# First attention: P divided by its sum on GpSimd ahead of the transpose, V as the stationary side of PV, and a new planner table

## The chip, the core and the metric

The kernel runs on one core of a Trainium2 chip. The metric is the time of one execution in device microseconds (us), taken as the median of several runs. The engines are named as in the profile: PE (TensorE: matmuls, transposes; PEld is its weight loads), DVE (VectorE), ACT (ScalarE), POOL (GpSimd) and SP (SyncE, which issues the loads).

## The reference

Two attention blocks share one shape and run over different caches. Their results are joined along the last axis.

```python
# B=16 batches, Sq=32 queries, D=1024, 32 query heads, Sk=1024 cached keys, Dh=128; all bf16
def block(x, k_cache, v_cache, wq, wo):
    q = heads(x @ wq)                                 # (B, 32, Sq, Dh)
    scores = einsum("bhqd,bhkd->bhqk", q, k) * Dh**-0.5
    p = softmax(scores)
    o = einsum("bhqk,bhkd->bhqd", p, v)
    return merge(o) @ wo                              # (B, Sq, D)
# A: 4 KV heads, each used by 8 query heads.   B: 32 KV heads, one for each query head.
return concatenate([A, B], axis=-1)
```

The K and V caches of B are 2 x 134 MB, those of A 2 x 17 MB, and the weights another 34 MB. Nearly all of the traffic is read once.

## The kernel before

**Units of work.** The first attention (A) is cut into 128 quads: one batch, four query heads and their 32 queries make 128 rows, against 1024 keys. `quadA_all` (L1239) lists the steps of one: the K tile is transposed on PE for every second quad (`st_ktrA`, L969), scores go to two PSUM banks (`st_scoresA`, L995), DVE takes the row maximum (`st_max`, L1038), ACT makes the exponential and its row sum (`st_exp`, L1051), PE transposes P in four pieces that each move two bf16 as one f32 (`st_ptr`, L1063), ACT or DVE copies that to SBUF (`st_pev`, `evac` L651), PE multiplies by V (`st_pvA`, L1083), DVE takes the reciprocal of the row sum (`st_recip`, L1165), ACT or DVE scales O by it (`st_norm`, L1174 or L1175), PE transposes O (`st_otr`, L1182), and the result is copied to `OTA_sb` (`evac` L651). In `st_pvA` the transposed P is the stationary side and V the moving one, so that O comes out with queries on the partitions, and `st_otr` has to turn it.

The second attention (B) is cut into 64 pairs of quads (`pairB`). Each takes four K tiles, which DVE transposes in 32x32 blocks (`st_ktrB`, L976), and four V tiles; its steps are `st_scoresB` (L1027), `st_max`, `st_exp`, `st_ptB` (L1097), `st_pvB` (L1116), `st_recip`, `st_norm` and `st_otr` (L1190). The last pair uses `st_last` (L1135, L1157) in place of `st_pvB` and what follows. Around both stand the projections of Q (`qprojA_head` L735, `qprojB` L754), the shuffle of Q for B (`qprepB_tr` L765, `qprepB_sh` L778) and the output projections (`oproj` L823, added up on DVE at L835, L844 and L839).

**The order.** `Prog.add` records every step with the buffers that it reads and writes. `list_schedule` then places all of them once, before the program is built: it keeps a planned time for each engine, takes durations from the table `DUR`, hands out the buffers of `SLOTS` (eight PSUM banks, two buffers of `P` and so on), chooses ACT or DVE for a step marked "any", and ranks what is ready by one of the 16 settings in `RANKS`. Which setting holds for each run of 77 steps is read from the table `TUNE`. What comes out is one fixed sequence for each engine, joined by semaphores. An engine works through its sequence in order, so a step that waits holds up all that stands behind it on that engine.

**The loads.** All loads are issued by SP, also in the planned order: KB (L910), VB (L955), KA (L891), VA (L898), weights (L714, L795, L805). A load waits until the last reader of its buffer is done, and the loads behind it wait with it. The outputs of all but the last group are issued by POOL (L847), the last by SP (L841).

The accumulated row sum and its reciprocal lie in `stat`, a buffer of eight slots with four columns, one slot for each quad:

```python
SLOTS = {"bank": 8, "P": 2, "P2": 1, "PT": 2, "PT2": 2, "stat": 8, "O": 2, "O2": 3}
```

## Time and profile before

| | |
|---|---|
| median of 3 runs | 852.57 us (852.47 to 854.04) |
| profiled execution | 851.34 us, of which the span from first to last instruction is 849.5 us |
| granted TensorE clock, mean | 0.995 |
| busy time | PE 783.0 us, DVE 727.0, ACT 623.6, POOL 6.1 |
| bytes moved | 341.68 MB, mean 402 GB/s |
| maximum, L1038 | 256 x 1210 ns on DVE |
| exponential, L1051 | 256 x some 1120 ns on ACT, and 205 ns each to read out the sum |
| K transposes of B, L976 | 256 x 1222 ns on DVE |
| norm of A, L1174 and L1175 | 123 x 378 ns on ACT, 5 x 327 ns on DVE |
| reciprocal, L1165 | 256 x 145 ns on DVE |
| copy of A's transposed O, L651 | 128x64 f32, 111 x 225 ns on ACT, 17 x 214 ns on DVE |
| transpose of A's O, L1182 | 128 matmuls, 225 ns each from start to end |

How to read it: the profile gives each instruction's duration from start to end. Matmuls overlap, so PE's own pace is read from the chain of waits, where each step is counted until the next. A duration on an engine costs time only where something later waits for it. The windows list, for a stretch of the span, the busy time of PE, PEld, DVE, ACT and POOL, the granted clock of PE, the DMA engines' share and GB/s.

### The profile page before, as it was taken

The numbers are of one execution on the slowest core, as the hardware profiler recorded it, in microseconds if no ns is written. First come the engines' busy times: TensorE is split into PE (matmuls) and PEld (weight loads), VectorE is DVE, ScalarE is ACT, GpSimd is POOL, SyncE is SP. The second block draws the span as 40 slices with busy tenths as digits, with TensorE's granted clock in tenths as the row PEclk, the third lists the DMA queues.
The fourth block names the chain that finished last, engine by engine and source line by source line (L and its number), as shares of the span: only waits on it lengthen the run. The fifth ranks groups of instructions, "written<-read, shape, count | busy, mean of one in ns | idle before, by whom it ended". The sixth has DMA issues, their size and how long they took to land.

```text
span 849.5 us, 29749 instructions
## 1 busy us (share of the span) xinstructions
PE 783.0 (92%) x13056; PEld 522.6 (62%) x13056; DVE 727.0 (86%) x1018; ACT 623.6 (73%) x1363; POOL 6.1 (1%) x20
## 2 busy tenths in 40 slices
PE   7989999999898999998999988999899998899878
PEld 4456665666565566665666665666666666666655
DVE  1499987979799898987999898998999978998995
ACT  3497787778677777786788787677877867686874
POOL 1000000000000000000000000000000000000000
PEclk9999999999999999999999999999999999999999
DMA  9999999999999999999999999999999999999995
GB/s 339 415 412 414 411 411 410 405 393 394 416 384 412 409 395 415 416 398 412 414 392 408 411 392 416 415 416 405 410 402 415 412 414 415 415 400 414 416 418 226
DMA packets 112208, 341.68 MB, mean 402 GB/s; under 512 B 12048, under 2 KB 12304, under 8 KB 112080
## 3 DMA queue, kind: packets, MB, share of 16 engines
q1 hardware_dynamic: 111520, 337.95, 100.0%
q8 instruction: 103, 1.69, 0.7%
q0 software_dynamic: 560, 1.84, 0.5%
q14 instruction: 25, 0.20, 0.1%
HBM read 337.64 MB, written 2.10 MB: 400 GB/s over the span
## 4 chain that ended last, share of the span: by engine, by line
PE 55%; DVE 23%; ACT 14%; DMA 5%; issue 2%; SPq 1%; DVEq 0%; ACTq 0%
DVE stat L1038 10%; PE psum L1116 10%; PE psum L823 10%; DVE KB_sb L976 8%; ACT P_sb L1051 8%; PE psum L1027 6%; PE psum L1063 5%; PE psum L754 5%; PE psum L1097 5%; PE psum L1083 4%; DMA KB_sb<-in_B_k_cache_dram 4%; PE psum L995 4%; PE psum L735 4%; ACT PT_sb L651 2%; ACT O_sb L1174 1%
## 5 line engine op out<-in xcount | busy, mean ns | idle before, releaser
L1038 DVE TENSOR_REDUCE stat<-psum 128x1 f32<-128x1024 f32 x256 | 303.6, 1210 | 50.7 <-PE psum L995 31.5
L1051 ACT ACTIVATE P_sb<-psum,stat 128x1024 bf16<-128x1024 f32 x246 | 275.9, 1122 | 63.2 <-DVE stat L1038 59.7
L976 DVE STREAM_TRANSPOSE KB_sb<-KB_sb 128x1024 f32<-128x1024 f32 x240 | 286.6, 1222 | 6.2 <-DMA KB_sb<-in_B_k_cache_dram 6.0
L651 ACT COPY PT_sb<-psum 128x512 f32<-128x512 f32 x226 | 131.4, 604 | 35.2 <-PE psum L1063 22.0
L1116 PE MATMUL psum<-VB_sb,PT_sb 64*64 64x256 bf16 x3584 | 116.2, 271 | 8.6 <-ACT P_sb L1051 5.2
L1116 PEld LDWEIGHTS psum<-VB_sb,PT_sb 64*64 64x64 bf16 x3584 | 97.0, 107 | 27.7 <-issue 25.5
L1174 ACT ACTIVATE O_sb<-psum,stat 128x128 bf16<-128x128 f32 (+1 forms) x205 | 80.8, 417 | 43.2 <-PE psum L1083 23.1
L1063 PE MATMUL psum<-id,P_sb 128*128 128x128 f32 x512 | 88.7, 297 | 6.9 <-ACT P_sb L1051 4.1
L1063 PEld LDWEIGHTS psum<-id,P_sb 128*128 128x128 f32 x512 | 74.0, 208 | 25.2 <-ACT P_sb L1051 13.8
L995 PE MATMUL psum<-KTA_sb,QT_sb 128*128 128x512 bf16 x256 | 84.4, 384 | 3.1 <-ACT P_sb L1051 1.6
L1083 PE MATMUL psum<-VA_sb,PT_sb 128*128 128x128 bf16 x1024 | 78.8, 221 | 7.5 <-ACT P_sb L1051 2.6
L1083 PEld LDWEIGHTS psum<-VA_sb,PT_sb 128*128 128x128 bf16 x1024 | 63.2, 99 | 31.6 <-issue 12.0
L1027 PE MATMUL psum<-KB_sb,QR 32*32 32x512 bf16 x3840 | 73.3, 394 | 8.1 <-ACT P_sb L1051 4.6
L1097 PE MATMUL psum<-id,P_sb 128*128 128x128 f32 x472 | 76.2, 287 | 4.1 <-ACT P_sb L1051 3.5
L754 PE MATMUL psum<-wq_sb,xT_sb 128*128 128x512 bf16 x256 | 72.4, 394 | 3.3 <-DMA wq_sb<-in_B_wq_dram 1.6
L1097 PEld LDWEIGHTS psum<-id,P_sb 128*128 128x128 f32 x472 | 63.8, 193 | 17.3 <-ACT P_sb L1051 7.5
L823 PE MATMUL psum<-woB_sb,OTB_sb 128*128 128x512 bf16 x256 | 66.9, 380 | 2.4 <-ACT P_sb L1051 1.7
L1027 PEld LDWEIGHTS psum<-KB_sb,QR 32*32 32x32 bf16 x3840 | 43.8, 89 | 35.3 <-ACT P_sb L1051 8.3
L823 PE MATMUL psum<-woA_sb,OTA_sb 128*128 128x512 bf16 x256 | 62.8, 380 | 0.4 <-ACT OTA_sb L651 0.3
L735 PE MATMUL psum<-xT_sb,wq_sb 128*128 128x512 bf16 x192 | 54.2, 380 | 1.7 <-issue 1.2
L1051 ACT ACTIVATION_READ_ACCUMULATOR P_sb<-psum,stat 128x1 f32 x246 | 50.3, 205 | 0.0
L835 DVE TENSOR_TENSOR acc<-acc,psum 128x512 f32<-128x512 f32 x64 | 41.3, 675 | 9.6 <-PE psum L823 9.4
(74 smaller groups left out, 720.2 us busy)
## 6 DMA issues: line engine op xcount, KB each, us to landing
KB_sb<-in_B_k_cache_dram SPq DMA_DIRECT2D x240, 512.0 KB, 8.9
VB_sb<-in_B_v_cache_dram SPq DMA_DIRECT2D x234, 512.0 KB, 7.8
KA_sb<-in_A_k_cache_dram SPq DMA_DIRECT2D x64, 256.0 KB, 7.8
VA_sb<-in_A_v_cache_dram SPq DMA_DIRECT2D x64, 256.0 KB, 8.0
wq_sb<-in_B_wq_dram SPq DMA_DIRECT2D x16, 512.0 KB, 8.3
woB_sb<-in_B_wo_dram SPq DMA_DIRECT2D x32, 256.0 KB, 8.5
woA_sb<-in_A_wo_dram SPq DMA_DIRECT2D x32, 256.0 KB, 7.0
wq_sb<-in_B_k_cache_dram SPq DMA_DIRECT2D x16, 512.0 KB, 11.5
```

The lines of the kernel that those rows point to most:

```text
L651: return e.copy(dst, src) if hasattr(e, "activation") else e.tensor_copy(dst, src)
L754: last = e.matmul(bank(v)[:, 0:CW], xT_sb[:, 1, j, G * P:(G + 1) * P], wq_sb[:, j, mh * CW:(mh + 1) * CW], start=(j == 0), stop=(j == DJ - 1))
L823: last = e.matmul(bank(v)[:, 0:OUTW], OT[:, gp, hh, :], wo_[:, hh, oh * OUTW:(oh + 1) * OUTW], start=(hh == 0), stop=(hh == nh - 1))
L976: pr.add("dve", lambda e: e.transpose(tile_k(x).bitcast(F32), tile_k(x).bitcast(F32)), writes=[home_k(x)], name="KBt_tr", rtag={home_k(x): ...
L995: pr.add("pe", lambda e, u=u: e.matmul(bank(vS[u]), qt[:, q.b, q.hh0:q.hh0 + 4, :].rearrange("p a q -> p (a q)"), KTA_sb[:, sl, u * 512:(u ...
L1027: last = e.matmul(bank(q.vS[g2])[32 * x:32 * x + 32, :].rearrange("p (s j) -> p s j", s=16), lhsT, rhs, start=(fp == 0), stop=(fp == 3), t ...
L1038: pr.add("dve", lambda e: e.tensor_reduce(stat[:, vst.idx, 0:1], both(vS), AXIS.XY, ALU.max, negate=True), writes=vS + [vst], name="max")
L1051: return e.activation(dst, src, ACTF.Exp, bias=stat[:, vst.idx, 0:1], scale=1.0, accum_out=stat[:, vst.idx, 1:2])
L1063: last = e.transpose(bank(vb)[:, m * P:(m + 1) * P], p32[:, m:Sk // 2:NPK], id32[:])
L1083: last = e.matmul(bank(vb)[:, 0:Dh], ptc_of(vPT, c, 0, P), VA_sb[:, kvs, c, :], start=(c == 0), stop=(c == NCH - 1))
L1097: last = e.transpose(bank(vb)[:, m * P:(m + 1) * P], p32[:, 4 * h + m:Sk:8], id32[:])
L1116: last = e.matmul(bank(q.vbo)[n0:n0 + 64, 0:2 * Dh].rearrange("p (i d) -> p i d", i=2), pt2_chunk(vPT, c, e0, n0), v2[e0:e0 + 64, :, c, :] ...
```

## The change

For the first attention, the reciprocal of the row sum is taken straight after the exponential, and POOL multiplies the 128x1024 P by it in place, ahead of the transpose. P gets three buffers. In `st_pvA` V becomes the stationary side and the transposed P the moving one, so that O comes out with the head dimension on the partitions: A's norm and the transpose of O are gone, and one copy of 128x128 takes O to `OTA_sb`.

Along with it: in B the two row sums of a pair share a slot of a new buffer `rs`, and one reciprocal serves both; the transpose of B's O has a moving side of 64 columns in place of 128; the shuffle of Q for B uses a stationary side of 64 columns (`idd`) and half as many matmuls, and the transpose ahead of it is made in place. The planner has other durations for these steps (1.2 us and 0.2 of hand-off for the multiplication), another table `TUNE`, and finer turns behind step 4466. As every step is placed anew, the order on each engine differs nearly throughout.

```diff
-SLOTS = {"bank": 8, "P": 2, "P2": 1, "PT": 2, "PT2": 2, "stat": 8, "O": 2, "O2": 3}
+SLOTS = {"rs": 4, "bank": 8, "P": 3, "P2": 1, "PT": 2, "PT2": 2, "stat": 8, "O2": 3}
...
-TUNE = (6, 7, 1, 5, 6, 8, 8, 8, 8, 8, 8, 11, 5, 15, 1, 9, 0, 1, 5, 1, 7, 14,
...
+TUNE = (12, 6, 6, 13, 3, 12, 12, 14, 4, 15, 6, 2, 15, 11, 15, 5, 15, 7, 14, 2, 0, 5,
...
+FINE = 4466
+FINE_WINDOW = 11
...
-            turn = len(order) // WINDOW
+            turn = len(order) // WINDOW if len(order) < FINE else FINE // WINDOW + (len(order) - FINE) // FINE_WINDOW
...
...
         def qprepB_tr(m_, G):
-            pr.add("dve", lambda e: e.transpose(QBt[:, :].bitcast(F32), Qtok[:, qs, :].bitcast(F32)),
+            pr.add("dve", lambda e: e.transpose(Qtok[:, qs, :].bitcast(F32), Qtok[:, qs, :].bitcast(F32)),
...
         def qprepB_sh(m_, G):
-                    for rg in range(4):
-                        last = e.matmul(out_[32 * rg:32 * rg + 32], ident[32 * a:32 * a + 32, 32 * a:32 * a + 32], src_[:, rg // 2, :, :],
-                                        start=True, stop=True, tile_position=(32 * a, 32 * rg))
+                    for hf in range(2):
+                        last = e.matmul(out_[64 * hf:64 * hf + 64], idd[32 * a:32 * a + 32, :], src_[:, hf, :, :],
+                                        start=True, stop=True, tile_position=(32 * a, 64 * hf))
...
         def st_exp(q):
-                return e.activation(dst, src, ACTF.Exp, bias=stat[:, vst.idx, 0:1], scale=1.0, accum_out=stat[:, vst.idx, 1:2])
+                return e.activation(dst, src, ACTF.Exp, bias=stat[:, vst.idx, 0:1], scale=1.0, accum_out=stat[:, vst.idx, 1:2] if q.pi == 0 else rs[:, q.vrs.idx, q.e:q.e + 1])
...
         def st_pvA(q):
-                    last = e.matmul(bank(vb)[:, 0:Dh], ptc_of(vPT, c, 0, P), VA_sb[:, kvs, c, :], start=(c == 0), stop=(c == NCH - 1))
+                    last = e.matmul(bank(vb)[:, 0:P], VA_sb[:, kvs, c, :], ptc_of(vPT, c, 0, P), start=(c == 0), stop=(c == NCH - 1))
...
         def st_otr(q):
             if q.pi == 0:
-                pr.add("pe", lambda e: e.transpose(bank(vb)[:, 256:320].bitcast(BF), O_sb[:, vO.idx, :], ident[:]), reads=[vO, "ident"], writes=[vb], name="OT_tr")
-                dst = OTA_sb[:, gp, q.hh0:q.hh0 + 4, :].bitcast(F32)[:, :, tb // 2:(tb + Sq) // 2]
-                src = lambda: bank(vb)[:, 256:320].rearrange("p (a q) -> p a q", a=4)
+                dst = OTA_sb[:, gp, q.hh0:q.hh0 + 4, tb:tb + Sq]
+                src = lambda: bank(vb)[:, 0:P].rearrange("p (a q) -> p a q", a=4)
             else:
-                        last = e.matmul(bank(vb)[:, 256:384], O2_sb[:, vO.idx, i, :], rowsel[:, i, :], start=(i == 0), stop=(i == 1))
+                        last = e.matmul(bank(vb)[:, 256 + 64 * i:320 + 64 * i].rearrange("p (t q) -> p t q", t=2), O2_sb[:, vO.idx, i, :], sel(i), start=True, stop=True)
...
         def quadA_all(q):
             st_exp(q)
+            st_recip(q)
+            pr.add("pool", lambda g: g.tensor_scalar(P_sb[:, vP.idx, :], P_sb[:, vP.idx, :], stat[:, vst.idx, 2:3], 1.0, ALU.mult, ALU.mult),
+                   reads=[vst, "idd"], writes=[vP], name="pnorm")
             st_ptr(q)
             st_pev(q)
             st_pvA(q)
-            st_recip(q)
-            st_norm(q)
             st_otr(q)
```

In the changed kernel's own numbering, the multiplication is L1270, the transposes of A's P are L1072, A's PV is L1092, B's PV is L1125, the K transposes of A are L977 and those of B L984, the reciprocals L1174 (A) and L1176 (B), the additions L843, L852 and L847.

## The prediction

> **What bounds the kernel now.** I read the page first: the shares, the slices and the chain.

> ```profile
> PE 783.0 (92%) x13056; PEld 522.6 (62%) x13056; DVE 727.0 (86%) x1018; ACT 623.6 (73%) x1363; POOL 6.1 (1%) x20
> ...
> DMA  9999999999999999999999999999999999999995
> ...
> PE 55%; DVE 23%; ACT 14%; DMA 5%; issue 2%; SPq 1%; DVEq 0%; ACTq 0%
> ```

> The DMA engines are busy in every slice but the last, while 55% of the chain runs through PE. Both hold: transfers fill the span, and PE decides where they pause. Next the windows of 5 us, whose last column is GB/s. Between 10 and 835 us there are 165; 151 move at least 395 GB/s, mean 412. The run moves 341.65 MB, which at 412 GB/s is 828.7 us. The other 20.8 us of the span are 3.7 us lost before 10 us, 7.5 us in the 14 slower windows, and 9.6 us after 835 us. Some of the slow windows:

> ```profile
> 190.00:195.00 5.00, 5.00 (x50) 3.09 (x42) 4.68 (x5) 4.93 (x11) 0.00 (x0) 1.00 0.97 335
> ...
> 230.00:235.00 5.00, 4.49 (x45) 2.82 (x46) 3.08 (x5) 1.70 (x6) 0.00 (x0) 0.66 1.03 409
> ...
> 240.00:245.00 5.00, 5.00 (x140) 3.48 (x109) 4.59 (x7) 3.78 (x8) 0.00 (x0) 1.00 1.00 351
> ...
> 435.00:440.00 5.00, 5.00 (x152) 3.87 (x152) 4.67 (x7) 3.87 (x9) 0.00 (x0) 1.00 0.99 349
> ```

> Where transfers starve, PE (second number) is busy throughout: it has fallen behind, once just after its granted clock dropped to 0.66. The waits of SP's queue say how that reaches the transfers: SP issues in order, and a load waits for PE to read out its buffer.

> ```profile
> SPq L955 <- PE psum L1116: 109.9, 36, 6.9
> SPq L891 <- PE psum L969: 80.9, 34, 6.7
> SPq L910 <- PE psum L1027: 57.0, 24, 5.1
> SPq L898 <- PE psum L1083: 54.2, 15, 8.3
> ```

> Most of these waits hide behind transfers already queued (a load lands some 8 us after its issue); only the excess is the 7.5 us. Last, the chain at the end:

> ```profile
> 840.50 1.95 PE psum L1135 x127
> ...
> 842.74 1.73 PE psum L823 x8
> ...
> 845.05 0.69 DVE acc L844
> 845.74 0.60 DVE woA_sb L839
> ```

> The last V tiles land near 840; after that come 128 matmuls, projections, two additions and the output: 9.4 us.

> **PE.** The chain gives occupancy (a step to the next), not latency. The 128 transposes of O (L1182, 0.06 us) go: -7 us. OT_trB keeps 252 matmuls (0.055 us each, 13.9 us), half as wide: between 0 and -7, taken -3.5, since a weight load of 99 ns beside each is unchanged. The Q shuffle drops from 16 to 8 matmuls in each of 32 groups; 16 took 0.61 us (0.28 and 0.30 plus a gap), so 19.5 us become between 9.8 and 19.5; I take -5, because each is twice as wide in output. PVA exchanges its sides at the same 128x128: 0, up to +2.6 us if the stride-2 stream costs what it costs L1027 against L823 (394 against 380 ns, 3.7% of 71.7 us). Sum -16 us, bounds -24 to -4, of some 764 us of PE occupancy.

> **ACT and DVE.** Of the norms for the first attention, ACT loses 123 x 378 ns = 46.5 us, DVE 5 x 327 ns = 1.6. OT_ev now writes 128x128, like the OTB_ev rows (282 ns against 225): +7.7 us with the five that move to ACT. 64 of 256 reciprocals go: 64 x 145 ns = 9.3 us off DVE. Counted over the new order, with the evictions the planner moved, ACT is 39 us lighter and DVE 10 us.

> **What the lighter engines are worth.** Weighted by the chain's shares: 16 x 0.55 + 10 x 0.23 + 39 x 0.14 = 16.6 us. The middle holds only 7.5 us of lost transfer time, so the rest cannot be had there. PE's relief is 2.1%, about 1 us in 50 us, and the lost stretches are 0.3 to 1.4 us each, so most should close; a new order will open a few elsewhere. I take 4.5 of 7.5, bounds +5 to -7.5.

> **The longer chain.** Between exp and transpose there are now a reciprocal on DVE and a multiplication on POOL. POOL's price is not in the trace. Its memsets of 128 and 256 elements took 200 and 311 ns: 0.87 us per 1000 elements, 0.98 us for 1024. Its affine select took 290 ns for 128 elements, 2.3 us at that rate. I take 1.2, nearer the memset, which like it streams whole rows; 0.98 and 2.3 are the bounds. 128 x 1.2 = 154 us on an otherwise idle engine. [...]

> PT_trA waits in PE's queue for this step; behind it stand scores, PV and projections of both attentions, hence SP's loads. I counted PE occupancy in program order between the last scores matmul and the first transpose of each quad: median 5.4 us before, 8.7 after. Before, that covers max 1.21 + exp 1.12 + accumulator read 0.2 + hand-offs 0.2 = 2.7 us; after, 0.145 + 1.2 + 0.1 more = 4.2. The surplus grows from 2.7 to 4.5 us; at 2.3 us it is still 3.4. Before, 10 quads of 128 had under 3 us; after, 3 have under 4.2, and 9 under 5.3. So I cost it at nothing; the cover is other quads' PE work, which the third buffer of P admits. Without it each quad would cost 1.4 us, 185 us in all. The reciprocal now stands early on DVE, with max and K transposes queued behind: that wait was 11.2 us in 13 cases, and I expect 10 to 25, absorbed by DVE's 10 us less work and its 14% idle. K and V of A stay held some 3.5 us of PE work longer (scores to the end of PVA, 9.1 to 12.7 us); that can delay L891 and L898 loads, and is in the +5. POOL's seven output DMAs (0.56 us each) now stand among the multiplications; a POOL wait for an accF could hold P back, but only in the last 160 us, some 1 us in all, bounds 0 to +2.

> A PSUM bank loses the norm, transpose and their hand-offs (0.38 + 0.22 + 0.1 us per quad): part of the same gain. Setup copies and the in-place Q transpose stand in the load phase or replace equal work: 0. The first 16 rows of SP are the same, so the 3.7 us stay.

> **The end.** Now 64 of L1135's 128 matmuls, with their projection, stand ahead of the other 64. The first half's V tiles are issued first; two tiles are 1.05 MB, 2.5 us at 412, and that half's work is 0.98 + 0.43 + 0.11 + 0.86 = 2.4 us. Behind the last landing are then 0.98 us instead of 1.95 and four projection matmuls less (0.86): -1.8 us if PE is in time. The addition L844 that stood between (0.69 us) comes earlier in the new order, but partly beside PE: up to 0.7 more. I take -1.5, as PE may be late, bounds -2.5 to +1.

> **Sum.** -4.5 - 1.5 = -6.0. The profiled execution took 851.34 us (span 849.5, 1.84 around it): 845.3. The median is 1.23 above it: 846.5.

> **Rivals.**
> No change: the new order makes as many pauses as it closes; PE already stands idle for 66 us of the span, and that could simply grow. For it: the DMA row is full everywhere. Against: pauses come where PE is full, and PE gets lighter. 852.5.

> [...]

> All pauses close: -7.5 and -2.5, 842.6. For it: 16.6 us of weighted relief. Against: the clock dip, which the change does not touch.

> That the change does not do what it says is excluded by the order: 128 multiplications on POOL, no L1182.

> **How the numbers follow.** Forecast 0.64, all close 0.10, no change 0.13, slower 0.13. A measurement here can tell about 0.2% (1.7 us) from no change. Faster 0.74, same 0.13, slower 0.13. The forecast's own range is 843 to 850.5. The range reaches down to 841.5, past all pauses closed, and up to 853.5, through no change; the slower case stays out.

> **What would show it.** Right: POOL near 160 us, about 1.2 us each; PE busy lower; L1072 waiting for POOL no longer than L1063 waited for exp (18.0 us); fewer than 14 windows under 395 GB/s; less than 9.4 us after the last tile. Wrong: multiplications or L984 transposes with two lengths (1.2 and above 1.8 us); PE idle before L1072; new slow windows with SP waiting for L1092 or L977.

## The result, and the profile after

The changed kernel takes 856.87 us (median of 13 runs), the kernel before 852.57 us beside it. The ratio is 1.0055, 95% interval 1.0034 to 1.0075. So it is slower by about 0.5%, where the forecast was 6 us faster, and the time lies above the range (841.5 to 853.5). The profiled execution took 856.87 us with a span of 855.0, against 849.5 before: +5.5 us.

First the page of the changed kernel: the shares of the engines, the slices of the DMA engines, and the chain by engine.

```profile
PE 756.5 (88%) x12552; PEld 514.9 (60%) x12672; DVE 725.5 (85%) x942; ACT 598.5 (70%) x1247; POOL 149.5 (17%) x151
...
DMA  9999999999999999999999999999999999999992
...
PE 54%; DVE 19%; ACT 13%; DMA 9%; issue 3%; SPq 1%; POOL 0%; DVEq 0%; ACTq 0%
```

PE and ACT are lighter, as forecast. (120 matmul records are missing: 12552 against 12672 weight loads. So PE's busy time is too low here, by an estimate of some 13 us: the kernel before with 53 small matmuls ahead of it, a run told below, lacks 126 records and shows 769.6 us for 783.0. PE is compared by its weight loads below.) "issue" went from 2% to 3%, which looks like nothing. The groups of GpSimd's multiplication and of DVE's K transposes:

```profile
L1270 POOL TENSOR_SCALAR P_sb<-P_sb,stat 128x1024 bf16<-128x1024 bf16 x128 | 142.8, 1117 | 657.6 <-DVE stat L1174 596.3
...
L984 DVE STREAM_TRANSPOSE KB_sb<-KB_sb 128x1024 f32<-128x1024 f32 x240 | 285.9, 1222 | 9.7 <-DMA KB_sb<-in_B_k_cache_dram 9.2
```

A multiplication takes 1.117 us. A K transpose takes 1222 ns, as before. Now the waits of PE, where "issue" is a wait for nothing that the profile shows:

```profile
PE psum L1036 <- issue: 5.8, 3, 2.7
...
PE psum L1125 <- issue: 4.8, 4, 2.2
...
PEld psum L1072 <- POOL P_sb L1270: 3.4, 7, 1.1
...
PE psum L1072 <- POOL P_sb L1270: 2.6, 2, 2.0
```

These columns are us in total, times and the longest; the last two lines are the waits for the multiplication. Behind the load phase the longest waits of PE have no releaser: up to 2.7 us, in the middle of `scoresB` (L1036) and `PVB` (L1125). The windows of 5 us that answer to the slow ones of before, some of 10 under 395 GB/s (before 14):

```profile
50.00:55.00 5.00, 5.00 (x119) 3.54 (x108) 2.93 (x4) 0.23 (x1) 0.39 (x1) 0.72 0.84 314
55.00:60.00 5.00, 2.61 (x23) 1.67 (x23) 4.92 (x8) 4.49 (x10) 0.34 (x1) 1.00 0.89 312
...
335.00:340.00 5.00, 3.24 (x40) 1.98 (x40) 3.08 (x8) 1.89 (x5) 1.12 (x1) 1.00 0.85 308
...
685.00:690.00 5.00, 4.95 (x46) 3.66 (x40) 5.00 (x6) 4.91 (x13) 1.11 (x1) 1.00 0.89 323
```

Before, PE was busy throughout such a window. Now the worst ones follow a half clock (0.72 at 50 to 55 us) or hold a hole in PE (2.61 and 3.24 of 5 us); in the last one shown PE is busy as before. Last, the chain of the last 45 us, three columns: start, us, what ran:

```profile
811.15 3.09 PE psum L831 x7
...
818.42 1.15 PE psum L1036 x38
819.58 1.35 issue
820.93 0.65 PE psum L1036 x5
...
835.87 1.15 PE psum L1036 x30
837.02 1.73 issue
838.75 0.43 PE psum L1036 x4
...
842.28 1.95 PE psum L1125 x64
```

Twice PE stops in the middle of one `scoresB` step. The last big tile has landed at 839.9 us, as early as before (840.5), but 15.1 us remain after it, against 9.1.

So the account of the +5.5 us is: after the last tile +6.0; the slow windows between 10 and 835 us lose 7.4 us, against 7.5; the rest is -0.4. The whole loss is at the end, and the middle gained nothing.

### The profile page after: what moved, and what is told of

It reads as the page before. It is cut to its first block, busy times and chain, and to the rows that moved or that the text cites. A ratio compares the mean times of both kernels' runs of the same rounds, so it can differ in the third digit from the quotient of the medians.

```text
span 855.0 us, 28882 instructions
## 1 busy us (share of the span) xinstructions
PE 756.5 (88%) x12552; PEld 514.9 (60%) x12672; DVE 725.5 (85%) x942; ACT 598.5 (70%) x1247; POOL 149.5 (17%) x151
## 3 DMA queue, kind: packets, MB, share of 16 engines
q0 software_dynamic: 560, 1.84, 0.5%
## 4 chain that ended last, share of the span: by engine, by line
PE 54%; DVE 19%; ACT 13%; DMA 9%; issue 3%; SPq 1%; POOL 0%; DVEq 0%; ACTq 0%
PE psum L1125 10%; DVE stat L1047 9%; PE psum L831 9%; ACT P_sb L1060 8%; PE psum L1036 7%; DVE KB_sb L984 7%; PE psum L1072 5%; PE psum L1092 5%; PE psum L1106 5%; PE psum L742 4%; DMA KB_sb<-in_B_k_cache_dram 4%; PE psum L761 3%; DMA VB_sb<-in_B_v_cache_dram 3%; PE psum L1003 3%; PE psum L977 2%
## 5 line engine op out<-in xcount | busy, mean ns | idle before, releaser
L984 DVE STREAM_TRANSPOSE KB_sb<-KB_sb 128x1024 f32<-128x1024 f32 x240 | 285.9, 1222 | 9.7 <-DMA KB_sb<-in_B_k_cache_dram 9.2
L1270 POOL TENSOR_SCALAR P_sb<-P_sb,stat 128x1024 bf16<-128x1024 bf16 x128 | 142.8, 1117 | 657.6 <-DVE stat L1174 596.3
L658 ACT COPY PT_sb<-psum 128x512 f32<-128x512 f32 x218 | 125.4, 596 | 39.9 <-PE psum L1106 21.9
L1125 PE MATMUL psum<-VB_sb,PT_sb 64*64 64x256 bf16 x3584 | 118.8, 276 | 12.9 <-issue 4.8
L1125 PEld LDWEIGHTS psum<-VB_sb,PT_sb 64*64 64x64 bf16 x3584 | 100.0, 109 | 32.9 <-issue 28.3
L1072 PE MATMUL psum<-id,P_sb 128*128 128x128 f32 x512 | 86.8, 295 | 9.1 <-ACT P_sb L1060 3.0
L1072 PEld LDWEIGHTS psum<-id,P_sb 128*128 128x128 f32 x512 | 73.9, 208 | 23.1 <-issue 15.2
L1036 PE MATMUL psum<-KB_sb,QR 32*32 32x512 bf16 x3840 | 75.6, 399 | 12.7 <-issue 4.0
L1092 PE MATMUL psum<-PT_sb,VA_sb 128*128 128x128 bf16 x1024 | 80.7, 222 | 6.9 <-ACT PT_sb L658 3.2
L1092 PEld LDWEIGHTS psum<-PT_sb,VA_sb 128*128 128x128 bf16 x1024 | 65.1, 98 | 28.7 <-ACT PT_sb L658 10.7
L1003 PE MATMUL psum<-KTA_sb,QT_sb 128*128 128x512 bf16 x208 | 67.4, 381 | 11.0 <-ACT P_sb L1060 5.3
L761 PE MATMUL psum<-wq_sb,xT_sb 128*128 128x512 bf16 x243 | 66.4, 388 | 4.7 <-DMA wq_sb<-in_B_wq_dram 2.7
L831 PE MATMUL psum<-woB_sb,OTB_sb 128*128 128x512 bf16 x226 | 60.4, 386 | 9.3 <-issue 2.0
L1036 PEld LDWEIGHTS psum<-KB_sb,QR 32*32 32x32 bf16 x3840 | 42.6, 89 | 41.2 <-issue 8.7
L831 PE MATMUL psum<-woA_sb,OTA_sb 128*128 128x512 bf16 x238 | 58.6, 379 | 2.4 <-issue 1.8
L1188 ACT ACTIVATE O_sb<-psum,rs 128x256 bf16<-128x256 f32 x81 | 36.4, 472 | 33.5 <-PE psum L1125 30.5
L742 PE MATMUL psum<-xT_sb,wq_sb 128*128 128x512 bf16 x182 | 49.2, 379 | 1.3 <-issue 0.6
## 6 DMA issues: line engine op xcount, KB each, us to landing
KB_sb<-in_B_k_cache_dram SPq DMA_DIRECT2D x240, 512.0 KB, 10.2
```

The lines of the kernel that those rows point to most:

```text
L658: return e.copy(dst, src) if hasattr(e, "activation") else e.tensor_copy(dst, src)
L831: last = e.matmul(bank(v)[:, 0:OUTW], OT[:, gp, hh, :], wo_[:, hh, oh * OUTW:(oh + 1) * OUTW], start=(hh == 0), stop=(hh == nh - 1))
L984: pr.add("dve", lambda e: e.transpose(tile_k(x).bitcast(F32), tile_k(x).bitcast(F32)), writes=[home_k(x)], name="KBt_tr", rtag={home_k(x): ...
L1003: pr.add("pe", lambda e, u=u: e.matmul(bank(vS[u]), qt[:, q.b, q.hh0:q.hh0 + 4, :].rearrange("p a q -> p (a q)"), KTA_sb[:, sl, u * 512:(u ...
L1036: last = e.matmul(bank(q.vS[g2])[32 * x:32 * x + 32, :].rearrange("p (s j) -> p s j", s=16), lhsT, rhs, start=(fp == 0), stop=(fp == 3), t ...
L1072: last = e.transpose(bank(vb)[:, m * P:(m + 1) * P], p32[:, m:Sk // 2:NPK], id32[:])
```

## The experiments

**What stops PE.** The page has a DMA queue of its own for instructions, with 100 packets of 16 KB each:

```profile
q8 instruction: 100, 1.64, 0.7%
```

The trace has 25,344 weight loads and matmuls and 425 separate wait instructions of PE, 25,769 for 100 packets; before, 26,442 for 103. So a packet is worth 257 to 258 instructions of PE, by estimate some 64 bytes each, which fits a queue that brings PE's program. The two stops of over 1 us shown above lie 512 instructions apart, and all nine of the changed kernel at whole multiples of 256 from each other, give or take one: at instruction 193 or 194 of a block of 256, counted along the trace. They end 1.2 to 1.5 us after a packet of this queue has landed. A packet lands 4.2 us (median) after PE has entered the block before it, while the loads of K and V keep the DMA engines full; once the last tile is there it lands after 1.7 us (before) and 2.3 us (changed). At no block end of the two traces does PE go on sooner than 1.2 us after the packet of the next block has landed; where it gets there earlier, it stops. Of the nine stops of the changed kernel, six come behind blocks that PE went through quickly, in 3.6 to 5.3 us. The other three (2.57, 3.28 and 1.76 us) come behind blocks of 6.0 to 8.4 us, whose packet landed only 7.4 to 8.8 us after the entry; why so late is open. Six of the nine lie in `scoresB` and `PVB`, groups of 64 small matmuls in 1.2 and 1.95 us; the others lie in L831 and L1072. A stop is counted below as a gap of over 0.5 us between two weight loads at such a place, 1.0 to 1.7 us after a landing. The changed kernel has 9 of 16.8 us in all, 4.75 us of them in its last 45 us; the kernel before has 9 of 10.7 us, the last one at 570 us.

The planner knows of these blocks (`FETCH_BLOCK`): it counts 252 planned instructions for each. In the built program the block ends of the last 50 us lie 84 planned instructions ahead of that count in the changed kernel, and 16 to 22 behind it in the kernel before. One reason: PE has 425 separate wait instructions now, 330 before; the planner does not count them.

**Half the clock, after a stop or a wait.** The granted clock in windows of the changed kernel, two pairs (last three columns: clock, DMA share, GB/s):

```profile
500.12:503.53 3.41, 1.70 (x14) 0.89 (x18) 3.41 (x5) 2.73 (x5) 1.08 (x2) 0.98 1.03 412
503.53:506.94 3.41, 3.41 (x64) 3.08 (x65) 2.24 (x2) 2.34 (x4) 0.07 (x1) 0.52 1.06 411
...
718.00:721.40 3.40, 1.73 (x72) 1.03 (x60) 1.46 (x4) 0.58 (x2) 0.00 (x0) 1.00 1.04 416
721.80:725.20 3.40, 2.56 (x45) 1.25 (x47) 1.26 (x2) 0.44 (x3) 0.00 (x0) 0.50 1.02 418
```

PE was busy for half of 3.41 us, and in the next 3.41 us its clock is 0.5. In the first pair PE had waited for ACT (0.98 and 0.55 us), in the second it had stopped at a block end (2.69 us). Every low step (a stretch at clock 0.5) of the changed kernel ahead of its last few us follows a stretch in which PE was busy for 34 to 49%. It has 23.9 us of them, the kernel before 6.8. Of the 23.9 us, 13.7 begin behind or in a stop, 10.2 behind waits for other engines. The longest single wait of PE ahead of each was 1.0 to 2.7 us. A low step takes 3.413 us, the one at 46 us twice that, and within each of the two traces they begin at whole multiples of 3.413 us from each other.

The theories: **F**, the places of the block ends cost the time, with the half clock behind the stops. **P**, the multiplication on GpSimd does. **O**, the new order of the end does.

### Moving the block ends (F against O), and a short multiplication (P)

Small matmuls ahead of all of PE's work (27 ns each) shift every block end and change no order:

```diff
+ first_pe = [op for op in ops if op.eng == "pe"][0]
...
+ if eng_name == "pe" and op is first_pe:   # 85, 43 or 53 times:
+     e.matmul(psum[0:32, 0, 0:32], ident[0:32, 0:32], ident[0:32, 0:32], start=True, stop=True, tile_position=(0, 0))
```

With 85 the block ends of the last stretch fall where the planner had them. What was expected, first of that kernel, then of the same with 43, of the kernel before with 53, and of a multiplication of 128 of the 1024 columns (which leaves out most of that step):

> The changed kernel with 85 small extra matmuls (32x32) at the start of PE's program, so that every later PE instruction stands 170 places further on; no other engine's order changes, nor PE's own behind them. Theory F (instruction fetch): PE's program arrives in blocks of 256 instructions, and the stalls of the changed kernel (0.87, 1.76 and 2.12 us in its last 45 us, 16.8 us in all nine) stand where a block ends in the middle of dense work; 170 places bring the block ends at the end of the program to where the planner's own count of 252 puts them. Then the three stalls at the end go, 4.7 us, and with them the half clock that followed (some 1.5 us): 850 to 852.5 us, ratio to before 0.997 to 1.000. Theory O (the new order of the end itself is longer): the stalls move but the end stays 17 us after the last tile: 855 to 858, ratio 1.003 to 1.007. Theory P (POOL's step holds PE): no change, 856 to 858.

> The same with 43 extra matmuls, 86 places: the control for the filling itself and for another phase of the blocks, one that no plan was made for. Theory F: other groups are hit, stalls of 8 to 20 us in all, and the time goes with what falls in the last 45 us: anywhere from 852 to 860 us, but different from the run with 85 by over 2 us. Theories O and P: within 1 us of the run with 85 and of the changed kernel, 855.5 to 858.

> The kernel before, with 53 small extra matmuls at the start of PE's program (106 places), which brings its block ends at the end as far from the planner's count as they are in the changed kernel (some 84 places early). Theory F: it gets stalls near its end that it did not have, 2 to 5 us slower than before: 854.5 to 857.5, ratio 1.002 to 1.006. Theories O and P: 852 to 853.5, ratio 0.999 to 1.001.

> The changed kernel with POOL multiplying only the first 128 of the 1024 columns of P (the rest stays undivided, so this leaves most of that step out); the order is the same on every engine. Theory P: POOL's 1.12 us is on the path, and taking some 0.9 us off each of 128 brings 3 us or more: below 853.5, ratio below 1.001. Theories F and O: within 1 us of the changed kernel: 856 to 858, ratio 1.004 to 1.0065, and the stalls of PE's program stand at the same instructions as in the changed kernel.

| kernel | median us | ratio to before, interval | stops us | half clock us | lost 10 to 835 us | after last tile |
|---|---|---|---|---|---|---|
| before | 851.55 | | 10.7 | 6.8 | 7.5 | 9.1 |
| changed, 85 | 852.32 | 1.001 (0.9991 to 1.0028) | 18.3 | 20.5 | 9.1 | 8.5 |
| changed, 43 | 857.33 | 1.0064 (1.0041 to 1.0087) | 20.7 | 20.5 | 14.5 | 11.5 |
| before, 53 | 854.72 | 1.0032 (1.0014 to 1.0051) | 14.3 | 6.8 | 9.8 | 10.4 |
| changed, short multiplication | 855.95 | 1.0051 (1.0029 to 1.0073) | 15.1 | 20.5 | 7.4 | 13.4 |

(The last four columns are of one profiled execution, that of "before" the one shown ahead; "lost" is what windows of 5 us under 395 GB/s fall short of 412.) With 85 the end is short again, although the stops are 18.3 us in all, more than the 16.8 of the changed kernel: what counts is where they lie. In its chain the stops are gone, and the same step, the last `PVB`, starts at 838.61 us instead of 842.28:

```profile
835.48 2.36 DVE stat L1050 x2
837.84 0.60 DVE PT_sb L661
838.43 0.09 DVE rs L1179
838.52 0.09 issue
838.61 1.94 PE psum L1128 x64
```

This refutes O, whose order is the same. A third of the time on GpSimd (374 ns each) leaves the two stops at the end (2.2 and 2.1 us) and the time: P is refuted. The kernel before gets slower too when its block ends are moved, by 3.2 us. It was expected to do so by stops near its end; none lies in its last 45 us, and its profiled execution (851.67 us) was the fastest of the twelve, so it does not show where the 3.2 us lie. And 43 left the changed kernel as slow as it was (ratio 1.0064 against 1.0055). With the end repaired, the changed kernel only equals the kernel before; where its lighter engines went is not told by this.

### The same table for both kernels

Both tables of ranks are tuned, each for its own kernel. With one rank throughout neither is; the work of the change still differs, and the order that the planner makes of it:

```diff
- TUNE = (12, 6, 6, 13, 3, 12, 12, ...
+ TUNE = (10,) * 100
```

> The kernel before with one rank (10) through the whole table of its planner instead of a tuned one; nothing else is changed, so all engines do the work of before. Without the tuned order I expect more pauses of the transfers: 855 to 880 us, with 10 to 35 us of transfer time lost between 10 and 835 us against 7.5. It is one half of a pair: see the changed kernel with the same table.

> The changed kernel with rank 10 throughout, the pair of the run before it. Theory W (the change's relief of PE, ACT and DVE is worth transfer time, and in the tuned pair the order and the places of the instruction-fetch stalls used it up): where the order is not tuned, pauses are longer and the relief counts, so this is 3 to 15 us faster than the kernel before with the same table. Theory N (the transfers are at their ceiling, relief is worth nothing): within 2.5 us of it. Theory H (the longer chain through DVE and GpSimd harms by itself): over 2.5 us slower. One pair alone can be off by some 5 us through its own order, so the two pairs are read together.

> The kernel before with rank 3 throughout: 855 to 880 us, for the same reason as with rank 10.

> The changed kernel with rank 3 throughout, the second pair. Theory W: 3 to 15 us faster than the kernel before with rank 3. Theory N: within 2.5 us. Theory H: over 2.5 us slower. Read with the first pair: W wants a mean of both differences at -3 us or beyond, H at +3 or beyond, N between them with both small; two large differences of opposite signs would say that the order's luck is larger than the work of the change.

| rank | before | changed | difference |
|---|---|---|---|
| 10 | 884.22, ratio 1.0368 (1.0338 to 1.0398) | 870.74, ratio 1.022 (1.0192 to 1.0247) | -13.5 us |
| 3 | 883.51, ratio 1.0369 (1.0334 to 1.0403) | 879.77, ratio 1.0326 (1.03 to 1.0353) | -3.7 us |

The first pair is clear; the intervals of the second overlap. The mean, -8.6 us, is as theory W (the relief is worth time) wants it, and speaks against harm by the change itself. But the two differences are 10 us apart, so the luck of an order is as large as the work of the change, and two orders do not show what that work is worth. The kernel before took more than the 855 to 880 us expected of it, both times.

### A new order for each, with the blocks counted as they are

The planner now has block ends 61.5 planned instructions earlier and 251.74 apart (65.5 and 252.82 in the kernel before), and each table was searched anew, twice for each kernel.

```diff
- FETCH_BLOCK = 252
+ FETCH_BLOCK = 251.74
+ FETCH_OFF = -61.5
```

> The changed kernel with a new order only: its planner now counts the blocks of PE's program where they really end (61.5 planned instructions earlier, 251.74 apart instead of 252), and the rank table was searched anew under that count; the block ends of the finished program lie within 10 instructions of the plan. The work is that of the changed kernel. Theory F+W (fetch stalls in the wrong places used up the relief): no stall of over 1 us in the last 40 us, 8.5 to 10 us after the last tile as in the kernel before, the middle loses no more than 7.5 us, so 845 to 851 us, faster than the kernel before by 1 to 6 us. Theory N (the transfers allow nothing better): within 2 us of the kernel before. Theory L (any new order is a lottery, and what the planner counts does not matter): 852 to 862 us like the four shifted kernels.

> A second order of the changed kernel, from another search under the same count; its block ends drift to 15 instructions from the plan towards the end. F+W: 846 to 852 us, perhaps 1 us worse than the first order because of the drift. N: within 2 us of the kernel before. L: anything from 850 to 862, with no relation to the first order.

> The kernel before with the same treatment: block ends counted where they are (65.5 planned instructions earlier, 252.82 apart), and a new table from a search of the same length. Its own table had been as wrong in the first half as that of the changed kernel, but right in the last fifth. F+W: stalls fall in number, 849 to 853 us, and the changed kernel with the same treatment stays 1.5 to 5 us ahead. N: both kernels come out equal. L: 850 to 860.

> A second order of the kernel before from another search under the right count (block ends within 6 instructions). F+W: 849 to 853 us, 1.5 to 5 us behind the mean of the two orders of the changed kernel. N: equal. L: unrelated to the others.

The changed kernel took 851.88 and 858.65 us, the kernel before 852.90 and 855.80, its own order 850.94 beside them. Stops fell to 7.2 and 10.4 us in the changed kernel, as F says, but no time was won against the kernel before: 34.1 and 30.7 us were at half clock, against 3.4 and 23.9 in the two of before. Of the three theories L, the lottery, comes closest: it misses one of its three ranges, by 0.1 us (851.88 for 852 to 862). F+W has one of the four times in its ranges, 852.90. Counting the blocks alone is not enough.

### The half clock in the plan as well

The planner now also halves PE's rate for 3.41 us where PE was busy for under 46% of the 3.41 us before, and both tables were searched under both rules. The 46% is a value chosen for the plan.

```diff
+ if st > 15.0 and st >= pe_slow[0] and busy < CLOCK_BUSY * CLOCK_WIN:
+     pe_slow[0] = st + CLOCK_WIN
+ oc += min(oc, max(0.0, pe_slow[0] - st) / 2)
```

> The changed kernel, only its order is new: the planner counts block ends where they are, and now also halves PE's rate for 3.41 us where PE was busy for under 46% of the 3.41 us before; the table was searched under both. Theory K (the relief of PE turns into idle stretches, after which the clock drops; that and the fetch stalls ate the gain): half-clock time falls from 24 to 34 us in the earlier orders of the changed kernel to under 17, no stall over 1 us in the last 40 us, and the time is 845 to 850 us, faster than the kernel before. Theory L (lottery): half-clock time and time as in the two orders without the clock rule, 851 to 859. Theory N (the transfers allow nothing better than the kernel before): half-clock time falls, but the time stays within 2 us of the kernel before.

> A second order of the changed kernel from another search under the same two rules. K: half-clock time under 20 us, 846 to 851 us. L: 851 to 859. N: within 2 us of the kernel before.

> The kernel before under the same two rules and a search of the same length. Its heavier PE leaves fewer idle stretches to avoid. K: half-clock time 3 to 10 us, 849 to 853 us, 2 to 5 us behind the changed kernel with the same treatment. L: unrelated. N: equal to the changed kernel with the same treatment, within 2 us.

> A second order of the kernel before under the same two rules. K: 849 to 853 us, 2 to 5 us behind the mean of the two orders of the changed kernel. N: equal within 2 us. L: unrelated.

| kernel | median us | ratio to before, interval | stops us | half clock us | lost 10 to 835 us | after last tile |
|---|---|---|---|---|---|---|
| changed, order 1 | 856.71 | 1.0072 (1.0048 to 1.0096) | 10.9 | 20.5 | 9.5 | 11.8 |
| changed, order 2 | 848.23 | 0.997 (0.9955 to 0.9985) | 0.6 | 3.4 | 6.9 | 7.6 |
| before, order 1 | 854.69 | 1.0051 (1.0031 to 1.0071) | 5.4 | 13.7 | 9.3 | 10.9 |
| before, order 2 | 855.33 | 1.0053 (1.0031 to 1.0074) | 5.3 | 13.7 | 10.7 | 12.3 |

Order 2 of the changed kernel beats both kernels: 848.23 us, 2.2 us under the kernel before. It is the one in which the rules did what they are for. From its page:

```profile
span 844.9 us, 28859 instructions
...
PE 753.7 (89%) x12552; PEld 511.4 (61%) x12672; DVE 728.1 (86%) x947; ACT 594.1 (70%) x1242; POOL 149.6 (18%) x151
```

The engines' work is that of the other orders. The difference is in the half clock and in PE's waits without a releaser, the largest group of which is now:

```profile
PE psum L848 <- issue: 3.5, 22, 0.2
```

That is 22 waits of at most 0.2 us at the output projection, where there had been 2.7 us at once. Theory K has one kernel for it; in the other three, 14 to 20 us at half clock remained, and their times missed what K expected; L's range (851 to 859) holds order 1 of the changed kernel. Whether order 2 is fast for its places or by luck was asked by moving its block ends, with 43 and 90 of the small matmuls:

> The second order with the clock rule, unchanged, but 43 small extra matmuls (32x32, written to a bank before its first use) at the start of PE's program, which move every block end by 86 instructions against the work. They add about 2 us of PE work in the load phase. Theory F+K (this order is fast because no block end lies in a dense stretch, so PE neither stalls nor drops its clock): stalls come back, 8 to 20 us in all, with half-clock time of 10 to 25 us, and the time rises by 3 to 8 us to 851 to 856. Theory L (this order is simply a good one): within 2 us of 848.2.

> The same order with 90 such matmuls, so every block end is moved by 180 instructions of 256. F+K: as with 43, 3 to 8 us slower than without, at other places. L: within 2 us of 848.2.

With 43 it takes 857.62 us (1.0076, 1.0054 to 1.0097), with 90 it takes 851.34 (1.0014, 0.9998 to 1.003): 9.4 and 3.1 us more, in the same order and with the same work but for the small matmuls (1.2 and 2.4 us; the dearer kernel has fewer, but of the 3.1 us they could be most). Stops are back at 11.9 and 10.4 us, half-clock time at 13.7 and 20.5 us. One of them stands in the chain of the kernel with 43, in `PVB` close to the end:

```profile
842.14 1.87 PE psum L1145 x63
844.01 0.95 issue
844.96 0.27 PE psum L1145
```

So order 2 is fast because of where its block ends lie: F is shown for it, by the kernel with 43 above all, and L, which wanted both within 2 us of 848.2, is refuted. Stops and half clock came back together, so what each costs is not told apart. Order 2 is also the best of eleven orders and places of the changed kernel in this document, so its 2.2 us do not measure what the change is worth.

Over the 16 profiled executions with tuned or searched orders, a line through the spans gives 0.34 us (standard error 0.09) for each us at half clock, and 2.5 us (1.7) for the work of the kernel before against the changed one at equal half-clock time. That is a correlation over orders, not an experiment, and the second number is hardly told from nothing.

## Why the prediction was wrong

**The end (-1.5, bounds -2.5 to +1) failed, and with it most of the sum.** It measured +6.0 in the profile. The step itself was right: where PE is not stopped, 8.5 (with 85) and 7.6 us (order 2) remain after the last tile, 0.6 and 1.5 us less than 9.1. But "if PE is in time" was tested against work only, and the sum has no term for PE's program coming late. PE came late by stops at block ends (4.75 us, of which two of 1.35 and 1.73 us are in the chain) and by the half clock behind them (L831: 3.09 us at 811 us).

**The middle (4.5 of 7.5) failed too.** 7.4 us are lost, against 7.5, so the term was -0.1 and not -4.5. Sorted by time, the loss behind a low step of the clock or behind a stop (within 15 us) went from 2.1 to 6.6 us, and the rest from 5.4 to 0.8. So, as far as nearness in time can tell, the old pauses, in which PE is backlogged, did close in this order, and pauses behind stops and low steps opened as large. In no order of the changed kernel did the middle lose less than 6.9 us, not even where stops and low steps were nearly gone. So no run shows that this term can be had at a tuned order.

**The clock dip was misread.** The window from 230 to 235 us in the prediction was taken for a dip of the clock that the change does not touch. The timeline of before has the cause just ahead of it:

```profile
230.42 0.52 PE L1116 MATMUL psum<-VB_sb,PT_sb 64*64 64x256 bf16 x12 [2.22 <-issue]
```

A stop of 2.22 us inside 64 dense matmuls, and then half the clock. The change does touch such places: it moves every later instruction. The 2% of "issue" in the chain were read over.

**PE (-16, bounds -24 to -4) was right in sum, in part by luck.** By the starts of weight loads, without gaps over 1 us, PE's work fell by 22 us, from 802 to 780. The terms: the Q shuffle gave 0 (23.9 us both times) where -5 was taken; OT_trB -6.5 (26.6 to 20.1) for -3.5; PVA +1.9 (71.8 to 73.7), inside 0 to +2.6; the O transposes, which had 19.1 us with the short waits behind them, are gone, where -7 was taken. The shuffle's missing 5 us were made up there. What was not in the sum: 95 more wait instructions at 51 ns, some 4.8 us between those starts.

**GpSimd and DVE were right.** The multiplication took 1.117 us for 1.2, between the bounds of 0.98 and 2.3. The group of L1072 shows 6.0 us of waits for it in all (2.6 of matmuls and 3.4 of weight loads), far under 18.0. One of them, 2.0 us at 669 us, stands at a block end and outlasts the multiplication by 0.8 us. Another 15.2 us of waits of its weight loads have no releaser; with the short multiplication these are 17.2 us, so its length does not make them. DVE waited 10.5 us for row sums (7.0 at L1174, 3.5 at L1176), within 10 to 25. The two lengths, listed as a sign that the prediction is wrong, did not come: the multiplications took 1107 to 1122 ns, and a K transpose 1222 ns before and after. 49 of the 256 transposes ran beside a multiplication, and took 1226 ns (median) against 1225 of the others. So the kernel is slower, but not by its multiplications.

**What would have shown it** was listed as windows and the time after the last tile. Fewer than 14 windows came true (10) without a gain; 15.1 us against "less than 9.4" was the sign that told.

**Not tried and open:** the shuffle and OT_trB undone one by one in a fixed order; why three of four orders planned against the half clock kept 14 to 20 us of it (the planner's times differ from the chip's, and it does not know where the low steps can begin: their grid of 3.413 us lies 2.14 us past the first instruction in the kernel before, 1.62 us in the changed one); and what holds the last 7 us of the middle.

## What to carry to other kernels

Here, while the loads filled the DMA engines, a block of PE's instructions landed 4.2 us (median) after the entry of the block before, and 1.7 to 2.3 us after it behind the last tile. Moving the block ends of order 2 with 43 small matmuls (1.2 us of work) cost 9.4 us, more than the 2.2 us by which that order beat the kernel before. So look for PE waits of 1 to 3 us without a releaser inside dense groups of small matmuls, and for half-clock windows behind them, before anything is explained by work. A few dummy matmuls at the start of the program show whether a result hangs on these places; it takes more than one number of them (the changed kernel's ratio went from 1.0055 to 1.001 with 85, and to 1.0064 with 43). Compare two versions of a kernel with a scheduler under one table too, or the tuning of each is measured along with the change.

## What the runs showed of the hardware

Low steps of the granted clock, at 0.5, lasted 3.41 us in these two traces, and one of them twice that. Cut all 20 traces behind their first 15 us into windows of 3.41 us, in step with the low ones: PE was busy for less than 40% of 34 windows at full clock, and a low one followed each time. From 40 to 50% it followed 26 of 43, from 50 to 60% 28 of 94, from 60 to 70% 8 of 210, and above 70% none.

DVE's transposes of 128x1024 f32 (1222 ns) did not get longer beside GpSimd's multiplications (1226 ns beside, 1225 alone). A multiplication of 1024 columns took 1117 ns and one of 128 columns 374 ns: 0.83 ns a column on top of 0.27 us.
